# Strassen's product for layer 2 one chunk earlier, in a kernel of sparse attention and a two-layer MLP

## The chip, the cores and the metric

The kernel runs on one core of one Trainium2 chip. The metric is the device time of that core in microseconds (us). The kernel before took 303.28 us, the median of 3 runs (302.64 to 303.31).

## The reference, cut to what matters

Attention with two kinds of masks feeds a two-layer network with a leaky activation. Batches 8, heads 8, 576 positions of 64 values; so 4608 tokens of 512 values, and a hidden width of 2048.

```python
def _attn_ref(q, k, v):
    scores = scale * np.matmul(q, k.transpose(0, 1, 3, 2))
    mask_local = (rel >= 0) & (rel < 32)                       # heads 0..3
    mask_strided = (rel >= 0) & (pos[None, :] % 32 == pos[:, None] % 32)   # heads 4..7
    scores = np.where(masks[None, :, :, :], scores, -1000000000.0)
    attn = np.exp(scores - np.max(scores, axis=-1, keepdims=True))
    attn = attn / (np.sum(attn, axis=-1, keepdims=True) + 1e-09)
    return np.matmul(attn, v)

def _moe_ref(x, w_in, w_out, alpha):
    h = x @ w_in                                                # layer 1: 512 -> 2048
    g = np.maximum(h, 0.0) + alpha * np.minimum(h, 0.0)
    return (g @ w_out).astype(np.float32)                       # layer 2: 2048 -> 512
```

## The kernel before

The program is one long list of instructions; each engine works through its own in order, and semaphores hold an engine where it needs another's result. The 4608 tokens go through the network in 9 chunks of 512. Chunk n runs layer 1 in 16 steps (`lin1_piece`, one block of 128 hidden units each: 4 matmuls of 512 columns) and then layer 2. Between the steps the program puts pieces of the attention of a later batch: score products, value products, transposes. A batch is four head pairs; pairs 8 to 11 are batch 2, which is computed during chunk 1.

Each layer-1 step goes to ScalarE (`neg`, the negative part) and then VectorE (`fin`, the activation, written to `gT` in f16):

```python
    def lin1_piece(n, m):
        ...
        neg = npool.tile([128, 512], F32, tag="neg", name="neg")
        keep(nc.scalar.activation(neg, hps, AF.Relu, scale=-1.0))
        def fin():
            keep(nc.vector.scalar_tensor_tensor(
                gTs[n][:, m, :], neg, oma[:, m : m + 1], hps, op0=ALU.mult, op1=ALU.add))
        late.append(fin)
```

Layer 2 has two forms. The plain one, for chunks 0 and 1, takes 16 steps of 4 matmuls of 512 columns; the step `part` needs the quarter `part` of w_out:

```python
    def lin2_piece(n, i):
        mt, part = i // 4, i % 4
        ...
        for kf in range(4 * part, 4 * part + 4):
            keep(nc.tensor.matmul(
                ops, gTs[n][:, kf, 128 * mt : 128 * mt + 128], wout16[:, kf, :],
                start=(kf == 0), stop=(kf == 15)))
        if part == 3:
            ...  # ScalarE copies the 128x512 result out, SyncE stores it
```

The other, for chunks 2 to 8, is Strassen's product in Winograd's form: g and w_out are cut into 2x2 quarters, and seven products of quarters take the place of eight. Each of 14 steps is 8 matmuls of 256 columns. It needs four sums of quarters of w_out, made once (the one with index 3 overwrites a quarter of w_out), and four sums of quarters of g for each chunk:

```python
    def w_sums(eng, which):
        w1, w2, w4 = wsum
        w3 = wq(0, 1)
        steps = {
            1: (w1, wq(0, 1), wq(0, 0), ALU.subtract),
            2: (w2, wq(1, 1), w1, ALU.subtract),
            3: (w3, wq(1, 1), wq(0, 1), ALU.subtract),
            4: (w4, wq(1, 0), w2, ALU.subtract),
        }
        for z in which:
            o, x, y, op = steps[z]
            keep(eng.tensor_tensor(o, x, y, op=op))       # 128 x 2048, f16

    def lin2_sums(n, i):
        p, mt = i // 2, i % 2
        if i == 0:
            ...
            g_sum(nc.vector, n, 1, 6, 8)                  # g_sum(engine, chunk, which sum, from, to)
            g_sum(nc.vector, n, 2, 0, 4)
            g_sum(nc.vector, n, 2, 4, 8)
        if i == (1 if quiet(n) else 2):
            g_sum(nc.vector, n, 4, 0, 8)
        if i == (2 if quiet(n) else 4):
            g_sum(nc.vector, n, 3, 0, 8)
        bank, lhs, rhs, first = (
            ("A", quad(g, 0, 0), wq(0, 0), True),
            ("B", gsum[0], wsum[0], True),
            ("A", gsum[1], wsum[1], False),
            ("B", gsum[2], wq(1, 1), False),
            ("A", gsum[3], wq(0, 1), False),
            ("C", quad(g, 0, 1), wq(1, 0), True),
            ("A", quad(g, 1, 1), wsum[2], False),
        )[p]
        ...  # 8 matmuls of 256 columns
        ...  # products 0, 1, 2, 6: ScalarE copies the bank out; 3, 4, 5: VectorE adds it; SyncE stores
```

The first sum of g is made in parts: its first three quarters in layer 1, on GpSimd, as their rows come ready, which needs the layer-1 steps in the order 0, 8, 1, 9, ...

In chunk 0, layer 2 is written out as a list in which the 16 plain steps (`M`) stand among the work of batch 1: transposes (`T`, tails `t`), casts (`C`, `V`, `O`), scores (`S`), masks (`K`), value products (`P`), output transposes (`X`), and loads (`I` calls a function). The change touches its first lines:

```python
    run([
        ("M", 0), ("M", 1), ("I", load_qk, 2, False, "q"), ("M", 4), ("M", 5), ("M", 2), ("M", 3),
        ("T", 3, "q"), ("V", 1, 1, "dve"), ("M", 6), ("I", load_qk, 2, False, "k"),
        ("C", 1, "q", 1, "dve"), ("t", 3), ("T", 3, "k"), ("M", 7), ("M", 8),
        ...
```

The loop of chunks 1 to 8; `acc` says how many pieces of attention follow each step, and `left` is their number for the chunk (20 for chunk 1):

```python
    for n in range(1, NCH):
        ab = attn_until(n + 1) if n + 1 < B else len(pieces)
        left = ab - pos["i"]
        acc = 0.0
        for i in range(32 if n == 1 else 30):
            second["on"] = i >= 16
            if i < 16:
                if n > 1:
                    lin1_piece(n, {13: 7, 14: 14}.get(i, 8 * (i % 2) + i // 2))
                    if i in (5, 9, 13):
                        g_sum(nc.gpsimd, n, 1, i // 2 - 2, i // 2)
                else:
                    lin1_piece(n, i)
                    if i == 9:
                        load_v(3, False)
            elif n == 1:
                lin2_piece(n, i - 16)
                if i in (18, 22, 26):
                    w_sums(nc.vector, ({18: 1, 22: 2, 26: 4}[i],))
            else:
                lin2_sums(n, i - 16)
                if n == 2 and i == 20:
                    w_sums(nc.vector, (3,))
            if n < B - 2 or i < 16 or i > 19:
                acc += left / (22.5 if n == 1 else 16 if n == B - 2 else 20.5) * (0.5 if i < 16 else 1.0)
            cnt = int(acc)
            acc -= cnt
            attn_n(cnt, ab)          # that many pieces; with none, one deferred exp or mask
```

Scores of a pair are made in two halves. ScalarE takes their exponential, and GpSimd multiplies each half by a mask (lines L437 and L444 of the profile); the second half's exponential and mask are deferred by a step or two.

Of the kernel before, what the change touches and what calls it, by code (L numbers as in the profile page):

```python
# [31 lines left out]
def kernel(  # L32
# [10 lines left out]
    nc = tc.nc  # L43
    keep = tc.keep_in_program_order

    B, H, S, D = q.shape
# [37 lines left out]
    def hbank():  # L84

        z = next(z for z in turn if z not in busy)
        turn.remove(z)
        turn.append(z)
        return banks[z]
# [80 lines left out]
    def load_v(b, strided):  # L170


        if strided:
            st = spool.tile([128, 2048], F16, tag="v", bufs=2, name="stv")
            keep(nc.gpsimd.dma_start(
                st[0:72, :].rearrange("p (h e) -> p h e", h=4),
                v[b, 4:8, :, :].rearrange("h (p t) d -> p h (t d)", t=8)))
            loaded[b] = st
        else:
            v16 = vls[b % 2]  # L180
            base = v[b, 0:1, 0:1, :]
            r0 = 32 if b < 2 else 0
            keep(nc.gpsimd.dma_start(
                v16[r0:128, :, 0:64],
                bass.AP(tensor=base.tensor, offset=base.offset - (32 - r0) * D,
                        ap=[[D, 128 - r0], [96 * D, 24], [1, D]])))
            cast16[(b, False, "v")] = v16
# [345 lines left out]
    for g in range(7, npair + 2):  # L533
# [30 lines left out]
        for i, (kind, fn) in enumerate(seq):  # L564
            extra = []
            if todo and i in nslots:
                left = len([z for z in nslots if z >= i])
# [3 lines left out]
            def run(fn=fn, extra=extra, g=g, c=c, kind=kind, lastp=(i == lastP), first=(i == 0)):  # L571
                fn()
                for b, pr in extra:
                    if pr in ("q", "k"):
                        cast_l(b, pr)
                        if b + 1 < B:
                            load_qk(b + 1, False, pr)
                        continue
                    cast_v(b, pr, "pool")
                    if pr == 1 and b + 1 < B:  # L580
                        load_v(b + 1, True)
                if kind == "Tk" and g % 4 == 3 and c + 3 < B:
                    load_tail(c + 3, False)
                if lastp:
                    if 4 * DX <= g - 1 < npair and pairs[g - 1].xd:
                        x_dma(pairs[g - 1])
                    if g % 4 == 3 and DX <= c + 1 < B:
                        transpose_d()
                    if g % 4 == 2 and DX <= c and c + 1 < B:
                        load_d(c + 1)  # L590
                    if g % 4 == 1 and DX < c and c + 1 < B:
                        load_v(c + 1, False)
                if first and 4 * DX <= g - 3 < npair and pairs[g - 3].xd and pairs[g - 3].strided:
                    x_copy(pairs[g - 3])
# [4 lines left out]
    def attn_until(b):  # L599

        return max(i for i, (g, _) in enumerate(pieces) if g == 4 * b + 3) + 1
# [16 lines left out]
    def lin1_mm(n, m, kks, first, last):  # L618
        if first:
            hcur[m] = hbank()  # L620
        hps = hcur[m]
        c0 = (512 * n) % RING
        parts = [(c0, 0, min(512, RING - c0))]
        if c0 + 512 > RING:
            parts.append((0, RING - c0, 512 - (RING - c0)))
        for kk in kks:
            for x, (src, dst, w) in enumerate(parts):
                keep(nc.tensor.matmul(  # L628
                    hps[:, dst : dst + w],
                    win16[:, kk, 128 * m : 128 * m + 128],  # L630
                    xT[:, kk, src : src + w],
                    start=(first and kk == kks[0] and x == 0),
                    stop=(last and kk == kks[-1] and x == len(parts) - 1),
                    skip_group_check=True,
                ))
        return hps

    def lin1_piece(n, m):
        if n not in gTs:
            gTs[n] = gpool.tile([128, 16, 512], F16, tag="gT", name="gT")  # L640
        if n == 0 and m < 3:
            hps = lin1_mm(n, m, (0,), False, True)
        else:
            hps = lin1_mm(n, m, (2, 3, 1, 0) if n == 1 else range(4), True, True)
# [8 lines that stand above are left out]
# [3 lines left out]
    def lin2_piece(n, i):  # L656
        mt, part = i // 4, i % 4
        if part == 0:
            ops_cur[mt] = hbank()
            busy.append(turn[-1])  # L660
            ops_cur[mt, "z"] = turn[-1]
        ops = ops_cur[mt]
        r0 = 512 * n + 128 * mt
# [5 lines that stand above are left out]
            osb = opool.tile([128, 512], F32, tag="osb", name="osb")  # L669
            keep(nc.scalar.copy(osb, ops))  # L670
            keep(nc.sync.dma_start(out[r0 : r0 + 128, :], osb))
            z = ops_cur[mt, "z"]
            busy.remove(z)
            turn.remove(z)
            turn.append(z)


    def quad(t, i, j):

        return t[:, 8 * j : 8 * j + 8, 256 * i : 256 * i + 256]  # L680

    def wq(i, j):

        return wout16[:, 8 * i : 8 * i + 8, 256 * j : 256 * j + 256]
# [13 lines that stand above are left out]
            keep(eng.tensor_tensor(o, x, y, op=op))  # L698

    def g_sum(eng, n, which, k0, k1):  # L700

        g = gTs[n]
        g1, g2, g4, g3 = gsum
        o, x, y, op = {
            1: (g1, quad(g, 1, 0), quad(g, 1, 1), ALU.add),
            2: (g2, g1, quad(g, 0, 0), ALU.subtract),
            3: (g3, quad(g, 0, 0), quad(g, 1, 0), ALU.subtract),
            4: (g4, quad(g, 0, 1), g2, ALU.subtract),
        }[which]
        keep(eng.tensor_tensor(o[:, k0:k1], x[:, k0:k1], y[:, k0:k1], op=op))  # L710
# [204 lines left out]
    def attn_n(n, end):  # L915
        for _ in range(n):
            attn_step(end)
        if n == 0:
            attn_step(0)
# [7 lines left out]
    for z in (3, 4):  # L927
# [8 lines left out]
        "I": lambda fn, *a: fn(*a),  # L936
    })
    run([
        ("M", 0), ("M", 1), ("I", load_qk, 2, False, "q"), ("M", 4), ("M", 5), ("M", 2), ("M", 3),
        ("T", 3, "q"), ("V", 1, 1, "dve"), ("M", 6), ("I", load_qk, 2, False, "k"),  # L940
        ("C", 1, "q", 1, "dve"), ("t", 3), ("T", 3, "k"), ("M", 7), ("M", 8),
        ("C", 1, "q", 0, "dve"), ("I", load_tail, 2, False), ("S", 6), ("C", 1, "k", 0, "dve"),
# [13 lines left out]
    for n in range(1, NCH):  # L956
        ab = attn_until(n + 1) if n + 1 < B else len(pieces)
        left = ab - pos["i"]
        acc = 0.0
        for i in range(32 if n == 1 else 30):  # L960
            second["on"] = i >= 16
            if i < 16:
                if n > 1:
                    lin1_piece(n, {13: 7, 14: 14}.get(i, 8 * (i % 2) + i // 2))
                    if i in (5, 9, 13):
                        g_sum(nc.gpsimd, n, 1, i // 2 - 2, i // 2)
                else:
                    lin1_piece(n, i)
                    if i == 9:
                        load_v(3, False)  # L970
            elif n == 1:
                lin2_piece(n, i - 16)
                if i in (18, 22, 26):
                    w_sums(nc.vector, ({18: 1, 22: 2, 26: 4}[i],))
            else:
                lin2_sums(n, i - 16)
                if n == 2 and i == 20:
                    w_sums(nc.vector, (3,))
            if n < B - 2 or i < 16 or i > 19:
                acc += left / (22.5 if n == 1 else 16 if n == B - 2 else 20.5) * (0.5 if i < 16 else 1.0)  # L980
            cnt = int(acc)
            acc -= cnt
            attn_n(cnt, ab)
        while pos["i"] < ab:
            attn_step(ab)
# [30 lines left out]
```

## Time and profile before

| | before |
|---|---|
| median of 3 runs | 303.28 us (302.64 to 303.31) |
| span of the profiled run | 300.8 us |
| TensorE clock granted | full throughout |
| chunk 1: layer 1 from, layer 2 from, end | 58.3, 74.3, 91.9 us |
| chunk 2: layer 1 from, layer 2 from, end | 91.9, 107.1, 123.3 us |
| w_out sums 1, 2, 4 on VectorE | start at 76.20, 81.47, 85.40 us |
| w_out sum 3 on VectorE | starts at 113.83 us |

How to read the lines of the profile: engines are PE (TensorE's matmuls), PEld (its weight loads), DVE (VectorE), ACT (ScalarE), POOL (GpSimd) and SP (SyncE). L758 is line 758 of the kernel: L628 is layer 1, L665 the plain layer 2, L758 Strassen's products, L650 the activation on VectorE, L698 the w_out sums, L710 the sums of g, L470 the value products, L481 their normalisation. In a timeline a line gives the start in us, the length in us (of several instructions where a count x2, x3 stands at the end), the engine, the line, the operation, what it writes and reads, and in brackets how long the engine had sat idle and what ended it. In the chain of waits a line gives start, length and what; only work that stood on the way to the end is in it. Matmuls are pipelined: the length of one matmul in a timeline holds its latency, so their cost is read from the chain, where they stand from start to start.

### The profile page before, as it was taken

What the parts mean: (1) busy time and instruction counts of PE and PEld (TensorE: products, weight loads), DVE (VectorE), ACT (ScalarE), POOL (GpSimd) and SP (SyncE); (2) the same over time, 40 slices, a digit from 0 to 9 for tenths busy, and PEclk for the clock granted to TensorE, in tenths of its full rate; (3) what the DMA queues carried; (4) which work ended last, traced back from release to release, by engine and by line L of the source; (5) the groups of instructions that cost most, each with busy time, mean ns of one, the idle gap of its engine ahead of it and who ended that gap; (6) DMA issues with size and microseconds to landing.
All of it is one profiled execution on the core that took longest, in us unless ns stands there. A gap on an engine that the chain in (4) does not pass through costs nothing.

```text
span 300.8 us, 7033 instructions
## 1 busy us (share of the span) xinstructions
PE 292.8 (97%) x2775; PEld 191.0 (63%) x2775; DVE 221.9 (74%) x422; ACT 179.8 (60%) x334; POOL 163.9 (54%) x173
## 2 busy tenths in 40 slices
PE   7899999999999999999999999999999999999995
PEld 2564456644544487647888887468745874784584
DVE  5698749779655988598848884888488958946872
ACT  3856548887557763776477746775576256506720
POOL 8862288169878866886497539772656003101300
PEclk9999999999999999999999999999999999999999
DMA  7999999999999974998499829971811040012004
GB/s 219 202 205 207 204 253 250 188 125 235 201 182 245 130 100 73 219 212 106 68 190 244 105 26 160 180 97 27 201 46 22 10 153 0 2 70 71 2 0 142
DMA packets 81202, 40.38 MB, mean 134 GB/s; under 512 B 58625, under 2 KB 76305, under 8 KB 81169
## 3 DMA queue, kind: packets, MB, share of 16 engines
q0 software_dynamic: 41728, 17.38, 47.7%
q1 hardware_dynamic: 39168, 22.03, 32.9%
q10 hardware_dynamic: 272, 0.52, 0.7%
q8 instruction: 22, 0.36, 0.5%
q14 instruction: 12, 0.09, 0.1%
HBM read 38.01 MB, written 9.44 MB: 158 GB/s over the span
## 4 chain that ended last, share of the span: by engine, by line
PE 83%; DVE 7%; DMA 5%; ACT 1%; POOL 1%; issue 1%; ACTq 0%; POOLq 0%
PE hb L628 39%; PE hb L758 26%; PE hb L665 6%; PE pv L470 4%; DMA ql<-in_q_dram 3%; DMA tl<-in_k_dram 2%; PE sp L422 2%; PE tp L255 2%; DVE x L481 2%; PE opl L758 1%; PE hx L628 1%; DVE gsum L710 1%; PE xp L489 1%; PE sph L422 1%; DVE et L330 1%
## 5 line engine op out<-in xcount | busy, mean ns | idle before, releaser
L628 PE MATMUL hb<-xT,win 128*128 128x512 f16 (+1 forms) x616 | 127.6, 357 | 0.0
L650 DVE SCALAR_TENSOR_TENSOR gT<-neg,oma,hb 128x512 f16<-128x512 f32 x138 | 100.7, 743 | 34.7 <-ACT neg L647 28.0
L647 ACT ACTIVATE neg<-hb 128x512 f32<-128x512 f32 x138 | 82.2, 597 | 35.6 <-PE hb L628 34.9
L628 PEld LDWEIGHTS <-win 128*128 128x128 f16 x640 | 59.8, 98 | 53.7
L437 POOL TENSOR_TENSOR et<-et,consts 128x576 f16<-128x576 f16 (+1 forms) x24 | 30.6, 1276 | 47.7 <-ACT et L435 39.0
L710 POOL TENSOR_TENSOR gsum<-gT 128x512 f16<-128x512 f16 x21 | 24.1, 1148 | 52.0 <-DVE gT L650 52.0
L758 PEld LDWEIGHTS <-gsum 128*128 128x128 f16 x448 | 41.6, 98 | 5.0 <-DVE gsum L710 0.2
L758 PEld LDWEIGHTS <-gT 128*128 128x128 f16 x336 | 31.5, 98 | 4.8
L481 DVE TENSOR_TENSOR x<-pv,rc 96x384 f16<-96x384 f32 (+2 forms) x62 | 33.0, 532 | 2.1
L444 POOL TENSOR_TENSOR et<-et,consts 128x576 f16<-128x576 f16 (+1 forms) x24 | 31.5, 1313 | 2.2 <-ACT et L441 2.2
L665 PE MATMUL hb<-wout,gT 128*128 128x512 f16 x128 | 31.5, 379 | 0.0
L470 PEld LDWEIGHTS <-et 72*128 72x128 f16 (+1 forms) x448 | 23.5, 98 | 11.0 <-DVE x L481 0.7
L770 ACT COPY o<-hb 128x512 f32<-128x512 f32 (+1 forms) x28 | 15.8, 564 | 24.1 <-PE hb L758 24.1
L758 PE MATMUL hb<-wout,gT 128*128 128x256 f16 x216 | 27.4, 273 | 0.0
L758 PE MATMUL hb<-wout,gsum 128*128 128x256 f16 x216 | 26.9, 273 | 0.0
L435 ACT ACTIVATE et<-sp 128x576 f16<-128x576 f32 (+1 forms) x24 | 15.5, 644 | 18.3 <-PE sp L422 18.3
L758 PE MATMUL hb<-wsum,gsum 128*128 128x256 f16 x216 | 26.0, 273 | 0.0
L773 DVE TENSOR_TENSOR o<-hb,o 128x512 f32<-128x512 f32 (+1 forms) x21 | 14.3, 679 | 14.7 <-PE hb L758 10.9
L479 DVE RECIPROCAL rc<-pv 72x6 f32<-72x6 f32 (+2 forms) x80 | 14.6, 182 | 9.6 <-PE pv L470 9.3
L441 ACT ACTIVATE et<-sph 128x288 f16<-128x288 f32 (+1 forms) x48 | 18.9, 409 | 0.0
L665 PEld LDWEIGHTS <-gT 128*128 128x128 f16 x128 | 11.0, 97 | 10.0
L470 PE MATMUL pv<-vs,et 72*128 72x65 f16 x256 | 15.6, 194 | 0.9 <-DVE vs L193 0.3
(110 smaller groups left out, 329.2 us busy)
## 6 DMA issues: line engine op xcount, KB each, us to landing
out_dram<-o SPq DMA_DIRECT2D x27, 256.0 KB, 4.0
kl<-in_k_dram SPq DMA_DIRECT2D x6, 512.0 KB, 7.5
ql<-in_q_dram SPq DMA_DIRECT2D x5, 512.0 KB, 6.8
stv<-in_v_dram POOLq DMA_DIRECT2D x8, 288.0 KB, 7.6
vl<-in_v_dram POOLq DMA_DIRECT2D x6, 384.0 KB, 10.6
win<-in_moe_w_in_dram POOLq DMA_DIRECT2D x4, 512.0 KB, 12.1
wout<-in_moe_w_out_dram POOLq DMA_DIRECT2D x4, 512.0 KB, 16.6
out_dram<-osb SPq DMA_DIRECT2D x8, 256.0 KB, 6.3
```

The lines of the kernel that those rows point to most:

```text
L437: keep(nc.gpsimd.tensor_tensor(mv, mv, m, op=ALU.mult))
L441: keep(nc.scalar.activation(ev[:, n * y : n * y + n], sps[y][0:r, 0:n], AF.Exp, scale=SCALE))
L444: keep(nc.gpsimd.tensor_tensor(mv, mv, m, op=ALU.mult))
L470: keep(nc.tensor.matmul(pv[:, 65 * x : 65 * x + 65], et[0:r, c : c + 128], v16[0:r, 2 * P.pr + hh, t, :] if P.strided else v16[:, 6 * (2 * ...
L481: keep(nc.vector.tensor_tensor(P.x16[0:w, c0 : c0 + 64 * nb].rearrange("r (c e) -> r c e", e=64), pvv[:, :, 0:64], rc[0:w, 0:nb].unsqueeze ...
L628: keep(nc.tensor.matmul(hps[:, dst : dst + w], win16[:, kk, 128 * m : 128 * m + 128], xT[:, kk, src : src + w], start=(first and kk == kks ...
L647: keep(nc.scalar.activation(neg, hps, AF.Relu, scale=-1.0))
L650: keep(nc.vector.scalar_tensor_tensor(gTs[n][:, m, :], neg, oma[:, m : m + 1], hps, op0=ALU.mult, op1=ALU.add))
L665: keep(nc.tensor.matmul(ops, gTs[n][:, kf, 128 * mt : 128 * mt + 128], wout16[:, kf, :], start=(kf == 0), stop=(kf == 15)))
L710: keep(eng.tensor_tensor(o[:, k0:k1], x[:, k0:k1], y[:, k0:k1], op=op))
L758: keep(nc.tensor.matmul(dst, lhs[:, kf, 128 * mt : 128 * mt + 128], rhs[:, kf, :], start=(first and own and kf == 0), stop=(kf == 7), skip ...
L770: keep(nc.scalar.copy(o, x))
```

## The change

Chunk 1 takes Strassen's product as well. For this the four w_out sums have to be there before: three are made on VectorE in layer 2 of chunk 0, one after its first two steps and two after its fourth, and the one that overwrites a quarter of w_out is made at the head of chunk 1, when chunk 0 is through with w_out. Chunk 1 then takes the same order of layer-1 steps, the same sums of g (but the third part of the first one on VectorE and not on GpSimd), and the same 14 steps of layer 2 as the chunks after it. Its attention is spread over 30 steps and no longer 32. The purpose is to run fewer matmul columns in layer 2 of chunk 1.

```diff
--- before.py
+++ after.py
@@ -936,7 +936,8 @@
         "I": lambda fn, *a: fn(*a),
     })
     run([
-        ("M", 0), ("M", 1), ("I", load_qk, 2, False, "q"), ("M", 4), ("M", 5), ("M", 2), ("M", 3),
+        ("M", 0), ("M", 1), ("I", w_sums, nc.vector, (1,)), ("I", load_qk, 2, False, "q"), ("M", 4), ("M", 5),
+        ("I", w_sums, nc.vector, (2, 4)), ("M", 2), ("M", 3),
         ("T", 3, "q"), ("V", 1, 1, "dve"), ("M", 6), ("I", load_qk, 2, False, "k"),
         ("C", 1, "q", 1, "dve"), ("t", 3), ("T", 3, "k"), ("M", 7), ("M", 8),
         ("C", 1, "q", 0, "dve"), ("I", load_tail, 2, False), ("S", 6), ("C", 1, "k", 0, "dve"),
@@ -957,27 +958,20 @@
         ab = attn_until(n + 1) if n + 1 < B else len(pieces)
         left = ab - pos["i"]
         acc = 0.0
-        for i in range(32 if n == 1 else 30):
+        if n == 1:
+            w_sums(nc.vector, (3,))
+        for i in range(30):
             second["on"] = i >= 16
             if i < 16:
-                if n > 1:
-                    lin1_piece(n, {13: 7, 14: 14}.get(i, 8 * (i % 2) + i // 2))
-                    if i in (5, 9, 13):
-                        g_sum(nc.gpsimd, n, 1, i // 2 - 2, i // 2)
-                else:
-                    lin1_piece(n, i)
-                    if i == 9:
-                        load_v(3, False)
-            elif n == 1:
-                lin2_piece(n, i - 16)
-                if i in (18, 22, 26):
-                    w_sums(nc.vector, ({18: 1, 22: 2, 26: 4}[i],))
+                lin1_piece(n, {13: 7, 14: 14}.get(i, 8 * (i % 2) + i // 2))
+                if i in (5, 9, 13):
+                    g_sum(nc.vector if n == 1 and i == 13 else nc.gpsimd, n, 1, i // 2 - 2, i // 2)
+                if n == 1 and i == 9:
+                    load_v(3, False)
             else:
                 lin2_sums(n, i - 16)
-                if n == 2 and i == 20:
-                    w_sums(nc.vector, (3,))
             if n < B - 2 or i < 16 or i > 19:
-                acc += left / (22.5 if n == 1 else 16 if n == B - 2 else 20.5) * (0.5 if i < 16 else 1.0)
+                acc += left / (16 if n == B - 2 else 20.5) * (0.5 if i < 16 else 1.0)
             cnt = int(acc)
             acc -= cnt
             attn_n(cnt, ab)
```

## The prediction, made before the result was known

> **What bounds the kernel now.** I read the page's busy shares first, then the chain of waits, then timelines of single stages.
>
> ```profile
> PE 292.8 (97%) x2775; PEld 191.0 (63%) x2775; DVE 221.9 (74%) x422; ACT 179.8 (60%) x334; POOL 163.9 (54%) x173
> ```
>
> TensorE (PE) is busy nearly everywhere, and the page gives 83% of the ending chain to it. Work taken off PE is therefore worth its full time, unless a wait takes its place. The chain (start, length in us, what) gives the price of both forms of layer 2, in the last chunks, where no attention is left:
>
> ```profile
> 245.17 13.81 PE hb L628 x64
> 258.99 12.23 PE hb L758 x112
> ```
>
> The reader is to see two rates. The first line is layer 1: 64 matmuls of 512 columns in 13.81 us, 216 ns each. The second is layer 2 by Strassen: 112 matmuls of 256 columns in 12.23 us, 109 ns each. The plain layer 2, which chunk 1 still has, is also 64 matmuls of 512 columns. The same chain marks where chunks 1, 2, 3 and 4 begin (first group of layer 1):
>
> ```profile
> 58.29 2.59 PE hb L628 x12
> ...
> 91.93 2.59 PE hb L628 x12
> ...
> 123.34 2.59 PE hb L628 x12
> ...
> 154.27 2.62 PE hb L628 x24
> ```
>
> So chunk 1 takes 33.64 us, chunk 2 31.41 and chunk 3 30.93. Chunk 1 minus its 2 x 13.81 us of dense matmuls leaves 6.02 us for attention. The attention groups that the chain lists inside it sum to 5.31 us (6 score groups, 11 value groups, 2 transposes, 1 output transpose), and six score groups are each followed by a matmul group about 0.1 us longer. That explains nearly all: chunk 1 holds no real PE stall. Chunks 2 and 3 hold the same operations but for one, the fourth w_out sum in chunk 2, and differ by 0.48 us. The chain shows why (this is the sum with index 3 in the code):
>
> ```profile
> 113.91 1.14 DVE wout L698
> 115.04 0.10 DVE rc L479
> 115.17 0.43 DVE x16s L481
> 115.65 0.36 PE pv L470 x6
> ```
>
> The sum holds VectorE (DVE); the normalisation of an earlier value product waits behind it, and the next value product on PE waits for that.
>
> [...] the w_out sums, 128x2048 of f16, took 1.21 us. [...] A mask on POOL that met a w_out sum lasted 2.25 us, against a mean of 1.31 for its line:
>
> ```profile
> 85.40 1.35 DVE L698 TENSOR_TENSOR wsum<-wout,wsum 128x2048 f16<-128x2048 f16 x1
> 85.64 2.25 POOL L444 TENSOR_TENSOR et<-et,consts 128x576 f16<-128x576 f16 x1
> ```
>
> while tail-load issues that met g sums (109.01 and 109.68 us in the timeline) took their usual 0.68 and 0.63 us.
>
> **The change part by part.**
>
> 1. Layer 2 of chunk 1 becomes Strassen: 13.81 - 12.23 = **1.58 us** less on PE, all on the path that sets the end.
>
> 2. The fourth w_out sum leaves chunk 2. Chunk 2 should become chunk 3: 31.41 - 30.93 = **0.48 us** less.
>
> 3. Three sums move into layer 2 of chunk 0. They cost 1.14 us each from start to start (as the sum in the chain above), 3.4 us. VectorE has just such a hole there:
>
> ```profile
> 35.76 0.75 DVE L650 SCALAR_TENSOR_TENSOR gT<-neg,oma,hb 128x512 f16<-128x512 f32 x1
> 40.53 0.69 DVE L193 COPY qT<-tp 128x512 f16<-128x512 f16 x1 [4.03 <-PE tp L255]
> ```
>
> From 36.5 to 40.5 us VectorE waits for PE, which runs 24 plain matmuls without a break. The second sum needs the last piece of w_out. GpSimd's queue tells when that lands: each of its later loads waits for the one eight places earlier, and the load whose wait ends on w_out at 37.09 us is eight behind the last w_out load:
>
> ```profile
> 37.09 0.64 POOL L165 DMA_DIRECT2D tl<-in_q_dram  x1 [1.44 <-DMA wout<-in_moe_w_out_dram]
> ```
>
> So the first sum runs from 36.5 to 37.7, the others can follow at once and end near 40.0, before 40.53. GpSimd only issues loads then. Cost: 0 us, at worst 0.3.
>
> 4. The fourth sum at the head of chunk 1 (1.2 us) falls into another hole:
>
> ```profile
> 58.33 0.22 DVE L193 COPY qT<-tt 128x128 f16<-128x128 f16 x1
> 59.97 2.32 DVE L650 SCALAR_TENSOR_TENSOR gT<-neg,oma,hb 128x512 f16<-128x512 f32 x3 [1.42 <-ACT neg L647]
> ```
>
> 58.55 to 59.97 is 1.42 us; its old readers on PE are done. Cost: 0.
>
> 5. Chunk 1 gets the sums of g. VectorE: 0.42 x 2 + 0.68 x 2 + 1.21 x 2 = 4.6 us, and three output adds of 0.69, 2.1 us; it loses three w_out sums, 3.8 us. Its 10.5 us busy in the 17.6 us of that layer become 13.4 in about 16. It has the room, but not the slack: in chunk 2 each sum ends a few tenths before PE needs it.
>
> ```profile
> 109.19 0.42 DVE L710 TENSOR_TENSOR gsum<-gT 128x512 f16<-128x512 f16 x1
> 109.53 1.28 DVE L710 TENSOR_TENSOR gsum<-gsum,gT 128x1024 f16<-128x1024 f16 x2
> 109.63 0.78 PEld L758 LDWEIGHTS <-gsum 128*128 128x128 f16 x8
> ```
>
> 6. GpSimd gets two sums of 1.15 us in layer 1 of chunk 1. It has none to give: in its timeline it runs from 63.68 to 74.16 us almost without a gap (two value casts, two load issues, masks). The first sum goes ahead of the fourth mask, the second ahead of a load issue and the fifth; later masks and the two casts for the next batch come up to 2.3 us later.
>
> 7. The attention of chunk 1 is paced faster: 20 pieces divided by 20.5 instead of 22.5. Counting it through, the second value product of pair 8 comes after the ninth layer-1 group instead of the tenth, so at 65.45 + 2 x 0.865 = 67.2 us. Its mask,
>
> ```profile
> 66.45 1.30 POOL L444 TENSOR_TENSOR et<-et,consts 128x576 f16<-128x576 f16 x1
> ```
>
> ends at 67.75 and can't be earlier, as it stands behind casts that wait for a load. **0.6 us** of PE stall.
>
> Sum without contention: 1.58 + 0.48 - 0.6 = 1.46 us. Now contention: with GpSimd 2.3 us late, its casts of q and k fall at about 76.5 to 78.6 us, just where VectorE wants its first g sums (near 77.0). [...] each may wait for a 1.04 us cast, and PE, needing the first at about 77.3, would stall up to 0.8 us; later waits are hidden, as the second sums need be ready only at 80.5. I take half, 0.4 us. Net gain 1.0 to 1.1 us: 303.28 - 1.1 = **302.2 us**.
>
> **The rivals.**
>
> A. Clean: PE loses 2.06 us and nothing comes back, 301.2 us. For it: the holes of steps 3 and 4 fit, and the same layer-2 code runs in chunk 3 without a visible stall. Against it: chunk 1 is where GpSimd is fullest.
>
> B. GpSimd becomes the bound of chunk 1: [...] only chunk 2's gain remains, 302.8 to 303.5. For it: the queue of step 6. Against it: the masks after the second are needed 2 us or more after they would be ready even when late, and GpSimd still has an idle gap of 3.06 us at 84.40 us in which to catch up.
>
> C. The w_out sums delay batch 1 in chunk 0. VectorE is busy 11.2 of the 12 us from 46 to 58 us, and the chain goes through it from 45 to 51 us; a sum running past 40.5 us would be paid for there, up to 1 us. Against it: they end about 0.5 us before the next copy, and the chain is held by the load of q until 42.06 us anyway. Time then: about 302.9.
>
> **Range and chances.** Between A and B lie 301.2 and 303.5 us; three runs of the kernel before spread over 0.7 us. I take 301.2 to 303.3. A change of 2% would be 6 us. The dense matmuls touched are 13.8 us long and the sums moved 5 us, so neither side can reach that short of a deadlock-like wait: 0.01 faster, 0.98 within, 0.01 slower.
>
> **What would show it.** Step 1: 112 matmuls of 256 columns in chunk 1, PE back to back. Step 2: chunk 2 at 30.9 us. Step 3: the three sums between 36.5 and 40.1 us and chunk 1 still starting near 58.3. Step 4: the fourth sum before 59.97. Steps 6 and 7: a wait of PE's value product on a mask near 67 us, and late casts of q and k. Contention: VectorE g sums near 77 us longer than 0.42 us, or weight loads waiting on them. The prediction is wrong if chunk 1 shortens by the full 1.58 us (A) or not at all (B), or if chunk 1 starts later (C).

## The result, and the profile after

The changed kernel takes **306.69 us** (median of 4 runs, 305.49 to 307.44) against 303.24 us: a ratio of 1.0114, interval 1.0076 to 1.0153. That is slower, and above the predicted 301.2 to 303.3 us. The profiled run is the 305.49 us one; its span is 303.7 us, 2.9 us more than before.

From the page of the changed kernel, the busy shares and the TensorE clock in 40 slices:

```profile
PE 293.4 (97%) x2823; PEld 196.7 (65%) x2823; DVE 230.7 (76%) x431; ACT 179.9 (59%) x334; POOL 165.8 (55%) x175
...
PEclk9999999999799999999999999999999999999999
```

PE runs 48 more matmuls, as Strassen's smaller ones should be, yet it is busy 0.6 us longer, not 1.6 us shorter. The 7 in the eleventh slice says why in part: there, between 76 and 84 us, the granted clock falls. Before, it was full throughout.

The chain of waits after (start, length, what) dates the stages and shows what the path went through:

```profile
58.47 2.59 PE hb L628 x12
...
74.38 2.48 DVE gsum L710
76.86 0.67 DVE gT L650
...
77.57 1.60 PE hb L758 x8
...
79.77 1.74 PE hb L758 x8
...
95.36 2.59 PE hb L628 x12
...
126.30 2.59 PE hb L628 x12
```

Layer 1 of chunks 1, 2 and 3 now begins at 58.47, 95.36 and 126.30 us (58.29, 91.93 and 123.34 before). So chunk 0 costs 0.18 us more, chunk 1 takes 36.89 us and not 33.64 (+3.25), chunk 2 takes 30.94 and not 31.41 (-0.47): together 2.96 us. All of the loss lies in chunk 1. There the end is held by a sum of g on VectorE (74.38 us, 2.48 us), then by an activation that waited behind it, and then by two Strassen products of 1.60 and 1.74 us for eight matmuls. At 109 ns a matmul they should take 0.87.

The timeline after, at the places of which the prediction spoke (start, length, engine, line, operation; in brackets the idle time ahead and its releaser):

```profile
36.82 2.48 DVE L698 TENSOR_TENSOR wsum<-wout,wsum 128x2048 f16<-128x2048 f16 x2
39.67 0.69 DVE L193 COPY qT<-tp 128x512 f16<-128x512 f16 x1 [0.37 <-PE tp L255]
...
58.65 1.22 DVE L698 TENSOR_TENSOR wout<-wout 128x2048 f16<-128x2048 f16 x1
60.15 2.33 DVE L650 SCALAR_TENSOR_TENSOR gT<-neg,oma,hb 128x512 f16<-128x512 f32 x3 [0.28 <-ACT neg L647]
...
66.64 1.29 POOL L444 TENSOR_TENSOR et<-et,consts 128x576 f16<-128x576 f16 x1
67.99 0.36 PE L470 MATMUL pv<-vl,et 128*128 128x65 f16 x6 [0.64 <-ACT neg L647]
...
74.06 1.29 POOL L437 TENSOR_TENSOR et<-et,consts 72x576 f16<-72x576 f16 x1
74.30 2.56 DVE L710 TENSOR_TENSOR gsum<-gT 128x512 f16<-128x512 f16 x1
75.29 1.28 POOL L444 TENSOR_TENSOR et<-et,consts 72x576 f16<-72x576 f16 x1
76.51 1.25 POOL L195 CAST ql<-ql 128x1024 f16<-128x1024 f32 x1
76.79 1.39 DVE L650 SCALAR_TENSOR_TENSOR gT<-neg,oma,hb 128x512 f16<-128x512 f32 x2
77.57 1.60 PE L758 MATMUL hb<-wout,gT 128*128 128x256 f16 x8 [2.34 <-DVE gT L650]
```

The w_out sums sit in the holes foreseen for them: the first of the three already starts at 35.56 us, the last two end at 39.3 us, and VectorE still idles 0.37 us before the copy at 39.67; the one in chunk 1 ends before the activation at 60.15. At 67.99 the value product waits 0.64 us. The profile puts this down to ScalarE, but the product starts 0.06 us after its mask ends (66.64 + 1.29), as it does in experiment 2, where the mask is named. Then comes the main event. At 74.30 us the third part of the first sum of g starts, an instruction that takes 0.42 us when alone, and lasts 2.56 us. It begins inside one mask of GpSimd (74.06 to 75.35) and ends 0.29 us after the next one (75.29 to 76.57) is over. The two activations queued behind it on VectorE start only at 76.79, and PE, which needs their gT for its first Strassen product, stands idle for 2.34 us.

The same stretch in windows of 2 us (stretch and its length, then busy us and instructions of PE, PEld, DVE, ACT and POOL, granted clock, DMA share, GB/s):

```profile
76.00:78.00 2.00, 0.43 (x4) 0.39 (x4) 2.00 (x3) 0.00 (x0) 2.00 (x3) 0.97 2.43 165
78.00:80.00 2.00, 2.00 (x24) 1.24 (x23) 1.93 (x6) 0.37 (x1) 2.00 (x3) 0.50 0.48 30
80.00:82.00 2.00, 2.00 (x19) 1.56 (x18) 2.00 (x2) 1.33 (x4) 1.85 (x3) 0.68 1.00 86
```

PE is nearly empty from 76 to 78 us, and when it has work again it has half the clock (0.50) for 2 us and a mean of 0.68 in the next 2. The account of chunk 1 is then: -1.58 (fewer columns), +0.64 (value product), +2.34 (wait for gT), +1.82 at the slow clock (products 0.73 and 0.87 us too long, a score group of 0.59 us that takes 0.37). The sum is +3.22 us, measured +3.25. These are the pieces of one run's chain; experiments 3 and 5 show runs with a full clock that gain nothing by it, so the last piece is not shown to be a loss of its own.

### The profile page after: what moved, and what is told of

It reads as the page before. It is cut to its first block, busy times and chain, and to the rows that moved or that the text cites. A ratio compares the mean times of both kernels' runs of the same rounds, so it can differ in the third digit from the quotient of the medians.

```text
span 303.7 us, 7141 instructions
## 1 busy us (share of the span) xinstructions
PE 293.4 (97%) x2823; PEld 196.7 (65%) x2823; DVE 230.7 (76%) x431; ACT 179.9 (59%) x334; POOL 165.8 (55%) x175
## 4 chain that ended last, share of the span: by engine, by line
PE 85%; DMA 5%; DVE 5%; ACT 2%; POOL 1%; issue 1%; ACTq 0%; POOLq 0%
PE hb L628 38%; PE hb L758 32%; PE pv L470 4%; DMA ql<-in_q_dram 3%; PE tp L255 2%; DMA tl<-in_k_dram 2%; PE sp L422 2%; DVE x L481 2%; PE hb L665 1%; PE opl L758 1%; PE hx L628 1%; PE xp L489 1%; PE sph L422 1%; DVE gsum L710 1%; ACT neg L647 1%
## 5 line engine op out<-in xcount | busy, mean ns | idle before, releaser
L650 DVE SCALAR_TENSOR_TENSOR gT<-neg,oma,hb 128x512 f16<-128x512 f32 x138 | 100.8, 744 | 33.6 <-ACT neg L647 26.8
L710 POOL TENSOR_TENSOR gsum<-gT 128x512 f16<-128x512 f16 x23 | 26.4, 1149 | 52.0 <-DVE gT L650 52.0
L758 PEld LDWEIGHTS <-gsum 128*128 128x128 f16 x512 | 47.4, 98 | 5.6 <-DVE gsum L710 0.2
L758 PEld LDWEIGHTS <-gT 128*128 128x128 f16 x384 | 36.4, 99 | 8.6 <-issue 2.6
L758 PE MATMUL hb<-wout,gT 128*128 128x256 f16 x248 | 32.8, 280 | 2.3 <-DVE gT L650 2.3
L770 ACT COPY o<-hb 128x512 f32<-128x512 f32 (+1 forms) x32 | 18.2, 568 | 25.0 <-PE hb L758 25.0
L758 PE MATMUL hb<-wout,gsum 128*128 128x256 f16 x248 | 31.0, 273 | 0.0
L758 PE MATMUL hb<-wsum,gsum 128*128 128x256 f16 x248 | 30.1, 272 | 0.0
L773 DVE TENSOR_TENSOR o<-hb,o 128x512 f32<-128x512 f32 (+1 forms) x24 | 16.3, 680 | 17.4 <-PE hb L758 13.6
L710 DVE TENSOR_TENSOR gsum<-gT 128x512 f16<-128x512 f16 (+1 forms) x17 | 15.6, 921 | 0.2
L665 PE MATMUL hb<-wout,gT 128*128 128x512 f16 x64 | 15.5, 379 | 0.0
```

The lines of the kernel that those rows point to most:

```text
L650: keep(nc.vector.scalar_tensor_tensor(gTs[n][:, m, :], neg, oma[:, m : m + 1], hps, op0=ALU.mult, op1=ALU.add))
L665: keep(nc.tensor.matmul(ops, gTs[n][:, kf, 128 * mt : 128 * mt + 128], wout16[:, kf, :], start=(kf == 0), stop=(kf == 15)))
L758: keep(nc.tensor.matmul(dst, lhs[:, kf, 128 * mt : 128 * mt + 128], rhs[:, kf, :], start=(first and own and kf == 0), stop=(kf == 7), skip ...
L770: keep(nc.scalar.copy(o, x))
```

## The experiments

Theory: a sum on VectorE and a GpSimd instruction that reads SBUF hold one another up where they meet. In the kernel before, a mask that met a w_out sum took 2.25 us, against a mean of 1.31 for its line; in the changed kernel the third part took 2.56 us beside two masks, and the fourth, of the same size, 0.42 at 79.56 us. The change puts such sums just where GpSimd, late by 2.3 us, has no gap, and PE waits behind them. Rivals: the w_out sums in chunk 0 do harm; the first stall (value product of pair 8) carries the rest; VectorE simply has too much to do; or the slow clock is the cause and not the sequel.

All ratios are against the kernel before on the same chip. "Two chunks" is the time in the profiled run from the first layer-1 matmul of chunk 1 to that of chunk 3 in the timeline: 65.05 us before, 67.83 in the changed kernel.

**1. The third part later.** It is joined to the fourth, at the head of layer 2, where PE needs it only after two steps.

```diff
-                if i in (5, 9, 13):
-                    g_sum(nc.vector if n == 1 and i == 13 else nc.gpsimd, n, 1, i // 2 - 2, i // 2)
+                if i in (5, 9, 13) and not (n == 1 and i == 13):
+                    g_sum(nc.gpsimd, n, 1, i // 2 - 2, i // 2)
...
-            g_sum(nc.vector, n, 1, 6, 8)
+            g_sum(nc.vector, n, 1, 4 if n == 1 else 6, 8)
```

> The change with one VectorE instruction moved: in chunk 1 the third part of the first sum of g (made after the 14th layer-1 step, where it lasted 2.56 us behind two GpSimd masks) is joined to the fourth part at the head of layer 2. Theory 1 ([...]that sum waits for GpSimd's masks and holds the activations behind it, PE then waits 2.3 us and its clock falls for 3 us more): the wait before the first Strassen product and the half-speed products go, 3 to 4 us; a new wait of up to 1 us may appear at the second product, as the joined sum now meets GpSimd's casts. Chunk 1 about 33 us in place of 36.9, time about 302.5. Rival 1 (GpSimd's late queue itself stalls PE): nothing moves, 306.5, since its queue is unchanged. Rival 2 (VectorE has too much work in chunk 1): nothing moves either, as the work is the same but for 0.2 us.

Measured: 305.81 us, 1.0091 (1.0059 to 1.0123); two chunks 68.19. The first product no longer waits and the clock stays full in the profiled run, but the time hardly moves: about 302.5 us was expected. The timeline of this kernel shows where it went:

```profile
78.67 4.54 DVE L710 TENSOR_TENSOR gsum<-gsum,gT 128x1024 f16<-128x1024 f16 x2
78.80 0.61 PE L758 MATMUL hb<-wsum,gsum 128*128 128x256 f16 x4 [1.04 <-DVE gsum L710]
```

The joined sum took 2.00 us beside the casts of q and k, and the next pair of sums 4.54 (1.29 when alone) beside two more masks; PE waited 1.04, 0.67 and 1.07 us for three products. So the single badly placed sum is not the whole cause: taken out of the way of the activations, the contention passes to the later sums.

**2. The third part on GpSimd,** as in the later chunks.

```diff
-                    g_sum(nc.vector if n == 1 and i == 13 else nc.gpsimd, n, 1, i // 2 - 2, i // 2)
+                    g_sum(nc.gpsimd, n, 1, i // 2 - 2, i // 2)
```

> The change with that third part on GpSimd, as in the chunks after it. Theory 1: VectorE no longer waits in front of its activations, so the 2.3 us wait and the slow clock go; GpSimd's second cast comes 1.15 us later and may cost a few tenths. Chunk 1 about 33 us, time about 302.5. Rival 1 (GpSimd's queue): GpSimd gets 1.15 us more, so the stall grows, time about 307.5. Rival 2 (VectorE's load): 0.42 us less there, time about 306.

Measured: 304.45 us, 1.0033 (1.0018 to 1.0047), better than the change, with the clock full, yet not better than before. In its profiled run (305.3 us) the casts of v began at 64.7 us and not at 63.9, as their load landed later, and the value product of pair 8 waited 1.88 us. The sums on VectorE again met the casts (a pair took 3.60 us), and the part on GpSimd was itself late by 0.80 us for PE.

**3. Filling PE's wait.** 11 matmuls of 512 columns, their result unused, stand ahead of layer 2 of chunk 1 and keep PE busy while it would wait.

```diff
             else:
+                if n == 1 and i == 16:
+                    fl = pspool.tile([128, 512], F32, tag="ps", name="fl")
+                    for _ in range(11):
+                        keep(nc.tensor.matmul(fl, ident, win16[:, 0, 0:512], start=True, stop=True))
                 lin2_sums(n, i - 16)
```

> The change with 11 more matmuls of 512 columns into a spare PSUM bank between layer 1 and layer 2 of chunk 1, where PE waits 2.3 us; their result is not used. They are 2.4 us at full clock. Theory 1 (the slow clock follows from the idle wait): the wait on VectorE stays, but PE is busy in it, the first 16 products run at 109 ns each and not at 200 ns and more; chunk 1 shortens by 1.5 to 1.9 us, time about 305. Rival 3 (the clock falls for another reason[...]): the products stay slow, time 306.5 or more.

Measured: 306.56 us, 1.0118 (1.0078 to 1.0157), no gain in time. In the profiled run (307.88 us) the load of v landed later still, at 65.9 us. There the wait at pair 8 was long, in the timeline:

```profile
70.04 0.36 PE L470 MATMUL pv<-vl,et 128*128 128x65 f16 x6 [2.30 <-POOL et L444]
```

and after it the clock was at 0.50 from 72 to 74 us. The window with the filler reads:

```profile
78.00:80.00 2.00, 2.00 (x12) 0.88 (x9) 2.00 (x3) 1.08 (x2) 2.00 (x3) 1.00 2.40 157
```

Full clock, and it stayed so in the 2 us after. The fall in this run came after the wait that was not filled, and none after the one that was. The slow clock is thus a sequel of the empty PE, not the first cause.

What it costs in time is another matter. The mean granted clock of a run tells whether it had such a fall: the three windows from 76 to 82 us in the changed kernel (0.97, 0.50 and 0.68) fall short of full clock by 0.06, 1.00 and 0.64 us, which takes 0.6% off (an estimate, 1.7 of 303.7 us). It is 0.993 or 0.994 in all four runs of the changed kernel; with the filler it is 0.994 in the profiled run and 1.00 in the other three. Those three had no fall, and still took 305.67 to 306.70 us, against 305.49 to 307.44 without the filler. The filler eats part of what it saves: the first product starts 1.30 us after the activations do (81.11 and 79.81 us), without it 0.78 us (77.57 and 76.79). That leaves some 1.3 of the 1.82 us to be gained, and no such gain is seen.

**4. The w_out sums alone,** in the kernel before: moved as in the change, the fourth to the head of chunk 2; chunk 1 keeps its plain layer 2.

```diff
-        ("M", 0), ("M", 1), ("I", load_qk, 2, False, "q"), ("M", 4), ("M", 5), ("M", 2), ("M", 3),
+        ("M", 0), ("M", 1), ("I", w_sums, nc.vector, (1,)), ("I", load_qk, 2, False, "q"), ("M", 4), ("M", 5),
+        ("I", w_sums, nc.vector, (2, 4)), ("M", 2), ("M", 3),
...
+        if n == 2:
+            w_sums(nc.vector, (3,))
```

(and the w_out sums in the loop are taken out)

> The kernel before with nothing but the w_out sums moved: 1, 2 and 4 into layer 2 of chunk 0 as in the change, 3 to the head of chunk 2; chunk 1 keeps the plain layer 2 and its order. Prediction's steps 2 and 3 (the holes of VectorE take the sums free, and the sum in layer 2 of chunk 2 cost 0.48 us): chunk 2 at 30.9 us, chunk 1 unchanged at 33.6, time about 302.8. Its rival C (the sums delay batch 1 in chunk 0): chunk 1 starts up to 1 us later, time 303.3 to 303.8.

Measured: 302.27 us, 0.9963 (0.9948 to 0.9978); chunk 2 takes 30.93 us, as chunk 3 does. This half of the change is a gain, and the first rival falls: the loss belongs to Strassen's product in chunk 1. (The sum at the head of chunk 1 is not in this test; the timeline above shows it in its hole.) The gain is 1.14 us, of which the trace places only the 0.48 us of chunk 2. Chunk 1 takes 34.30 us in the profiled run and not the expected 33.6: the casts of v began at 64.15 us (63.68 in the kernel before), and the value product of pair 8 waited 0.50 us. Where the rest of the gain comes from is not shown.

**5. The casts of v later.** GpSimd's casts of v for batch 2, which wait for a load, go behind the masks of the next pair, in the changed kernel.

```diff
-... if g % 4 == 0 and 8 <= g < npair else []
+... if g % 4 == (1 if c == 2 else 0) and 8 <= g < npair else []
```

> The change with GpSimd's two casts of v for batch 2 (and the next load of v) moved four layer-1 steps later in chunk 1, behind the second mask of pair 8, so that this mask no longer stands behind a cast that waits for a load landing at 63.5 to 65.9 us. Theory: the first stall of chunk 1 (the second value product of pair 8, 0.64 us in the profile of the change, 3 us where the load landed at 65.9) goes in full. GpSimd's work is the same in sum, so the third part of the g sum on VectorE still meets masks near 74 us and PE still waits about 2 us there with a slow clock after it: chunk 1 about 36.2 us in place of 36.9, time about 305.5, and less spread. Rival (the casts are not what holds the mask): the stall near 67 us stays.

Measured: 305.28 us, 1.0075 (1.0052 to 1.0097). The value product of pair 8 no longer waits. The third part still took 2.62 us between the same two masks, and PE, from the timeline:

```profile
76.82 1.03 PE L758 MATMUL hb<-wout,gT 128*128 128x256 f16 x8 [2.40 <-DVE gT L650]
```

The second rival falls too: without the first stall the second is there as before. One thing is odd: this wait of 2.40 us was not followed by a slow clock (8 matmuls in 1.03 us, and 1.00 in each window of 2 us from 76 to 82).

The other runs of this kernel tell more. Two of the eight have a mean clock of 0.994 and took 305.18 and 305.45 us; the six with a full clock took 304.67 to 305.74. With or without the fall, the time is the same. A likely reason, not tested: at full clock PE comes sooner to the later sums and waits for them. In this profiled run it waits 0.84 us at 82.61 us for a sum; in that of the changed kernel, after the slow clock, it waits for none.

**6. The meeting by itself,** in the kernel before, where chunks 3 and 4 have the same sums and a quiet GpSimd. In chunk 3 GpSimd gets four products that read SBUF, in chunk 4 twelve fills that only write it. Nothing uses the results.

```diff
                 lin2_sums(n, i - 16)
+                if n in (3, 4) and i == 17:
+                    for _ in range(4 if n == 3 else 12):
+                        if n == 3:
+                            keep(nc.gpsimd.tensor_tensor(junk, win16[:, 0, 0:576], win16[:, 1, 0:576], op=ALU.mult))
+                        else:
+                            keep(nc.gpsimd.memset(junk, 0.0))
```

> The kernel before with extra work on GpSimd alone in chunks 3 and 4, just when VectorE makes the g sums, where GpSimd is else idle: four products of two SBUF tiles of 128x576 in chunk 3, twelve memsets of the same tile in chunk 4; nothing uses the result. Theory 1[...]: in chunk 3 the five g sums of VectorE take 5.2 us or more, some of them over 2 us each, and PE waits, so the chunk grows by 1 to 4 us; in chunk 4, where GpSimd only writes, the sums keep their 0.42, 0.68 and 1.21 us and the chunk its 31.1 us. Rival 2 (in chunk 1 the sums were slow for another reason, as transfers or VectorE's load): both chunks keep 30.9 and 31.1 us.

Measured: 305.61 us in its one run; chunk 3 takes 33.79 us (30.93 before), chunk 4 31.08 (31.08 before). The timeline:

```profile
140.67 6.04 POOL L982 TENSOR_TENSOR junk<-win 128x576 f16<-128x576 f16 x4
140.82 1.40 DVE L710 TENSOR_TENSOR gsum<-gT 128x512 f16<-128x512 f16 x1
...
174.56 7.57 POOL L984 MEMSET junk<- 128x576 f16 x12
174.75 0.43 DVE L710 TENSOR_TENSOR gsum<-gT 128x512 f16<-128x512 f16 x1
```

VectorE has the same sums in both chunks, and GpSimd is busy for longer in chunk 4 (7.57 us against 6.04). Beside instructions that read, the first sum takes 1.40 us in place of 0.42, and the pair after it 3.44 in place of 1.29; beside fills, 0.43 and 1.29. This shows VectorE's half of the theory, and that the same sums cost PE nothing in chunk 4, where GpSimd does not read. Against the third rival, VectorE's load, this speaks for chunk 4; experiment 9 settles it for chunk 1, whose VectorE work it leaves in place.

**7 to 9. A quiet GpSimd where the sums are.** If the theory holds, Strassen in chunk 1 must pay once GpSimd reads nothing while VectorE makes the sums. All three take the edit of experiment 1. In number 7 the casts of q and k for batch 3 go to ScalarE, and no attention (so no masks) stands in the first four steps of layer 2. Number 8 adds the edit of experiment 5. Number 9 is number 8 with only the first two steps free. The edits of 9 (7 has `1.22 if i > 19`):

```diff
                     if pr in ("q", "k"):
+                        if c == 2:
+                            continue
                         cast_l(b, pr)
...
+            if n == 1 and i in (16, 17):
+                cast_l(3, "qk"[i - 16], "act")
+                load_qk(4, False, "qk"[i - 16])
-            if n < B - 2 or i < 16 or i > 19:
+            if n == 1 and i >= 16:
+                acc += 1.12 if i > 17 else 0.0
+            elif n < B - 2 or i < 16 or i > 19:
```

> The change with GpSimd kept free of reads while VectorE makes the g sums of chunk 1: the third part of the first sum at the head of layer 2, the casts of q and k for batch 3 on ScalarE in the first two steps of layer 2, and no attention piece in the first four steps of layer 2, so that the masks of pair 11 come after the sums. Theory 1: the sums keep 0.68 to 1.21 us, PE finds them ready; what is left is the stall of pair 8 near 67 us. Chunk 1 about 33 us in place of 36.9, time about 301.8 to 302.8. Rival 2 (VectorE's load): its work is the same, denser at the end; chunk 1 stays above 35 us.

> Both: GpSimd kept free of reads during the g sums, and the casts of v behind the mask of pair 8. Theory: both stalls go; chunk 1 near the 32.1 us that dense matmuls and attention need without a wait (33.64 less 1.58), time about 301.0 to 302.0, faster than the kernel before. Rivals: as for the parts; if layer 2's later steps, now fuller of attention, bring a wait of their own, chunk 1 stays at 33 us or more.

> As the last kernel (GpSimd free of reads during the g sums, casts of v behind the mask), but only the first two steps of layer 2 of chunk 1 are kept free of attention and not four, so that the last pieces end one step earlier. Theory: what the last kernel lost where chunk 2 starts (its first matmuls waited 1.3 us for the last transposed attention output, copied late by ScalarE) goes or shrinks; the masks of pair 11 now meet the last two g sums, which have a slack of over 2 us, so no wait there. Chunks 1 and 2 together 63.3 to 64.0 us, against 65.05 before and 67.8 in the change; time 301 to 302. Rival (the masks cost as much as they save): together 65 us or more, time about 303.

| | time, us | ratio (interval) | two chunks, us |
|---|---|---|---|
| 7 | 304.39 | 1.0050 (1.0033 to 1.0067) | 66.11 |
| 8 | 303.04 | 1.0000 (0.9985 to 1.0014) | 65.14 |
| 9 | 301.55 | 0.9947 (0.9928 to 0.9966) | 63.79 |

In 7 the sums are clean (0.69, 1.29 and 1.21 us), but the time missed its mark: the value product of pair 8 waits 0.82 us, and the start of chunk 2 waits 0.31 and 0.95 us for transposes that ScalarE copies late, because the attention was crowded into the end of the chunk. In 8 the first of these is gone, but with the second still there its time misses the expected 301.0 to 302.0 as well; in 9 the second is gone too. Number 9 beats both kernels. The w_out sums alone (experiment 4) have 0.9963 (0.9948 to 0.9978), and the two intervals overlap: what Strassen's product in chunk 1 adds to that gain, these times do not show. In its timeline one wait is left:

```profile
76.69 0.61 PE L760 MATMUL hb<-wsum,gsum 128*128 128x256 f16 x4 [0.40 <-DVE gsum L712]
```

**10. The casts back on GpSimd,** all else as in number 9.

```diff
-                        if c == 2:
-                            continue
                         cast_l(b, pr)
...
-                cast_l(3, "qk"[i - 16], "act")
-                load_qk(4, False, "qk"[i - 16])
```

> The same, but the casts of q and k for batch 3 stay on GpSimd, as in the change, where they come near 76 to 78 us on top of the first g sums. Theory 1: the first two or three sums wait for a cast of 1.04 us each and PE with them; 1 to 2 us slower than the kernel with the casts on ScalarE. Rival (only masks, which come in pairs back to back, matter; a single cast is absorbed): within 0.4 us of it.

Measured on the same chip as number 9: 305.2 us, 1.0066 (1.0045 to 1.0088), 3.65 us slower than 9; two chunks 68.66. More than expected. The timeline:

```profile
75.06 1.04 POOL L195 CAST ql<-ql 128x1024 f16<-128x1024 f32 x1
75.22 1.43 DVE L710 TENSOR_TENSOR gsum<-gT 128x1024 f16<-128x1024 f16 x1
...
78.73 3.90 DVE L710 TENSOR_TENSOR gsum<-gT,gsum 128x2048 f16<-128x2048 f16 x1
79.03 1.29 POOL L437 TENSOR_TENSOR et<-et,consts 72x576 f16<-72x576 f16 x1
```

The first sum meets a cast and takes 1.43 us (0.69 in number 9), and PE waits 1.14 us for it (0.40 in number 9). VectorE comes to the next large sum 3.51 us after the start of the first one (1.93 in number 9) and meets both masks of a pair. Its record begins ahead of theirs, but its length is about that of both masks and itself, 1.29 + 1.27 + 1.22 = 3.78 us; in number 9 it was the mask that waited (1.86 us in place of 1.29). PE then waits 2.24 us for a normalisation queued behind the sum, and the clock is at 0.54 after that. Two casts of a microsecond set off all of this.

**11 and 12. Two variants of number 9:** the attention packed more densely (1.25 in place of 1.12), and the casts of v ahead of the masks again (the edit of experiment 5 left out).

> The fastest kernel so far (GpSimd free of reads, casts of v behind the mask, two steps without attention) with the attention of layer 2 of chunk 1 paced at 1.25 pieces a step and not 1.12, so that the last piece comes one step earlier. Theory: the wait of 0.95 us where chunk 2 starts, for the last attention output copied by ScalarE, goes, and nothing else: time 0.5 to 1 us less. Rival (PE waits for ScalarE's and GpSimd's work as a whole in this dense stretch): the wait moves to a value product, time the same within 0.3 us.

> The fastest kernel so far with GpSimd's casts of v for batch 2 back in front of the masks of pair 8, as in the change. Theory: the stall of the second value product of pair 8 returns, 0.6 us where the load of v lands at 63.5 us and up to 3 us where it lands at 65.9; time 0.6 to 2 us more, with more spread. Rival (the other changes leave room for it): within 0.3 us.

Measured: 301.87 us, 0.9975 (0.9955 to 0.9995), and 302.98 us, 1.0005 (0.9989 to 1.0021). Denser packing shows no gain over number 9; a wait of 0.46 us at the start of chunk 2 was there. With the casts of v early the value product of pair 8 waits for its mask again, 0.99 us, and the kernel is level with the one before: that order gives the gain back.

## Why the prediction was wrong

**The step that failed is the contention term of the last sum,** "I take half, 0.4 us", with its bound of "up to 0.8 us". Measured in the profiled run were 2.34 us of wait and 1.82 us of slow clock after it: 4.16 us. The 1.82 belongs to this run's chain; as a loss in time it is not shown, since the runs of experiments 3 and 5 with a full clock were no faster for it.

The term was mis-sized in three ways. First, in the place: it looked at the sums in layer 2 (near 77 us) beside a cast. The third part, still in layer 1, was counted in step 5 as 0.42 us of room, and not held against GpSimd's timeline, although step 6's own delay of 2.3 us puts the masks of pair 10 there: they start at 71.64 and 72.87 us in the kernel before, so at about 73.9 and 75.2 when late. Second, in the length: it allowed each sum one other instruction, of 1.04 us. Behind two masks back to back the sum took 2.56 us (2.62 in experiment 5). Third, in what waits: not only the sum's own reader, but the activations queued behind it on VectorE, which PE needed at once. The slow clock was in no step at all.

Point by point:

- **Step 1** (1.58 us off PE): it agrees with the account of chunk 1, which closes to 0.03 us with it, and eight products take the 0.87 us of its rate where the clock is full. As a gain in time it is not shown by itself: experiment 9 is not clear of experiment 4.
- **Step 2** (0.48 us): right, 0.47 measured, and 30.93 us for chunk 2 in experiment 4.
- **Steps 3 and 4** (holes for the w_out sums, cost 0): right. Chunk 1 starts 0.18 us later, by as much as the cast that waits for the load of q (42.26 and not 42.08 us).
- **Step 5** (VectorE has the room): true as a sum of busy time, and of no use. Experiment 6 ran the same sums in chunk 4 with GpSimd writing only, and nothing was lost; the room was not what counted.
- **Step 6** (GpSimd 2.3 us late): right. The cast of q starts at 76.51 us; before, at 74.09.
- **Step 7** (0.6 us at pair 8): 0.64 measured, with some luck. It hangs on when the load of v lands: in the profiled runs the waiting casts began between 63.5 and 65.9 us, and where they began at 65.9 the wait was 2.30 us (not the 3 us of the expectations of experiments 5 and 12). In experiment 4 the wait was 0.50 us without the faster pacing.
- **Rival B** named the right engine, but as a queue that is late; it was dismissed since late masks are needed late. The masks were indeed early enough. What hurt was that they met a sum on VectorE: it took 2.56 us beside two of them and 0.42 alone, and in experiment 6 it was instructions that read, not fills, that lengthened such a sum (1.40 and 0.43 us).

Two things stay open. A wait of 2.40 us (experiment 5) left the clock alone, while those of 2.34, 2.30 and 2.24 us were followed by 0.50 to 0.54. Nor do the traces tell when VectorE waits for two GpSimd instructions and when for one. In experiment 6 four products stood back to back, and the first sum still got in after one of them (1.40 us). In experiments 1 and 10 a sum began 1.02 and 0.30 us ahead of a mask and still ended after it: in experiment 10 it took 3.90 us, and in experiment 1 its reader on PE could start only 2.92 us after the sum did (81.59 and 78.67 us).

## What to carry to other kernels

Moving work between engines, lay the timelines of VectorE and GpSimd over one another at the place in question: a short sum on VectorE can cost not only its own length but also that of the one or two reading GpSimd instructions that it meets (here 0.42 us became 1.40 beside products and 2.56 beside two masks), and what stands behind it in VectorE's queue waits as long (PE waited 2.34 us for the activations there). If the sums cannot be moved, clear GpSimd there. Four edits together turned 1.0114 into 0.9947: the third part joined to the fourth, the casts of q and k on ScalarE, two steps without masks, and the casts of v behind the masks; without the last of them the gain was gone (1.0005). And test each half of a change alone: the w_out sums by themselves had 0.9963, most of that gain.

## What the runs showed of the hardware

**A VectorE sum can wait through two GpSimd instructions.** 0.42 us became 2.56 behind two masks of 1.28; 1.22 us became 3.90 with two masks beside it. In experiment 6 it was one: 0.42 became 1.40 behind a product. Beside fills it stayed at 0.43. The prediction allowed a sum one instruction; the first two lengths are those of two.

**The clock fell after some waits of PE and not after others.** Three waits of 2.24 to 2.34 us were followed by 0.50 to 0.54, one of 2.40 was not (1.00, experiment 5), and neither was one of 1.88 us (experiment 2, a mean of 1.0 for the profiled run). After each of the three the windows of 2 us fall short of full clock by about 1.7 us in sum (0.97, 0.50 and 0.68 in the changed kernel, 0.65 and 0.50 in experiment 3, 0.54 and 0.60 in experiment 10). One and the same kernel had the fall in some runs and not in others: two of eight in experiment 5, three of six in experiment 10, by the mean clock. In experiment 10 the runs with it took 305.17 to 306.21 us and those without 304.85 to 305.23, in experiment 5 there was no difference. So it is not the length of the wait alone which decides; what else does, no run here shows.
